# A convolution in the Winograd manner: the first block's outer taps and the parameters loaded through GpSimd's queue

## The chip, the cores and the metric

The kernel runs on one core of a Trainium2 chip. The metric is the device time of one execution in microseconds (us). The engines are TensorE (PE; its weight loads are PEld), VectorE (DVE), ScalarE (ACT), GpSimd (POOL) and SyncE (SP), which issues most of the transfers. A transfer ("DMA") is issued by an engine into that engine's queue and carried out by 16 DMA engines. Memory beside the engines holds 128 rows (partitions).

## The reference

A 1-D convolution over the sequence with three taps, 1024 channels in and out, batch 2 and sequence 2048, then batch normalisation with given statistics, then SiLU. Cut to what matters:

```python
def reference(x, w, mean, var, g, b):          # x (2, 2048, 1024), w (3, 1024, 1024), bf16
    xp = jnp.pad(x, ((0, 0), (1, 1), (0, 0)))
    y = sum(jnp.einsum('bsc,cd->bsd', xp[:, k:k + S, :], w[k]) for k in range(3))
    inv_std = 1.0 / jnp.sqrt(var + 1e-5)
    y = (y - mean) * (g * inv_std) + b
    return _silu(y)
```

## The kernel before

**The method.** The convolution is done in tiles of 6 outputs from 8 inputs. Three steps make it up. First the input is transformed: each window of 8 positions becomes 8 values (`NJ`), by products with a small constant matrix `rm`. Then the taps are transformed: for each block of 128 output channels (`dc`, 0 to 7) the three taps `w0`, `w1`, `w2` become eight sets of weights; two of the eight are `w0` and `w2` as they are, the other six (`u`) are sums and differences of `w0`, `w2`, their multiples by 4, and `w1` or its double. Last, for each block and batch (a `Unit`), eight products over the 8 tiles of 128 input channels (`ct`) are added up in PSUM, and VectorE and ScalarE combine them into 6 outputs and apply scale, offset and SiLU.

**The input transform.** `load_x` (L99) loads one tile of 128 input channels of one batch, 512 KB; tiles 0 and 1 of the first batch come as two halves, the first half on SP's queue and the second on ScalarE's. There are `XBUFS` = 6 buffers. `Jobs.do` (L226) multiplies six or four windows at a time (16 windows a tile) at L231, and ScalarE (L249) or VectorE (L251) copies the result out of PSUM into `T_sb`. Which engine copies and which PSUM banks are used is written out by hand in `ORDER` (L29), which also says where products of the first unit (`First`, L398) are mixed in, and where a few products on zeros fill in (`z5`). `load_small` (L94) loads the 48 rows of input that the tiles leave over; for the second batch it is cut into 15, 26 and 7 rows.

**The taps of the first block.** `load_w` (L107) loads taps of one block into `raw[dc]`, laid out as three taps beside each other in each row. For block 0 it loads tap 0 and tap 2 as two transfers of 256 KB right behind input tile 2, and tap 1 behind input tile 7; other blocks come as one transfer of 768 KB. All are on SP's queue. GpSimd makes the six sets `u` of block 0: `prepare_first` (L167) first forms three sums `e` from `w0` and `w2` (L137, L129), then with tap 1 the six results (L150). `prepare_second` (L183) does block 1, with some help by ScalarE, and `prepare_w` (L152) the later ones.

**The scales.** `scales` (L206) stands ahead of that on GpSimd. It waits for the parameters `prm` (var, g, mean, b: 128 rows of 64 bytes, L524) and computes scale and offset with six operations on 8 elements a row, one of them a power (L211).

**The order.** Nothing is reordered by a scheduler: each engine runs its instructions in the order of the program. A transfer on SP's or ScalarE's queue also waits for the landing of the transfer eight issues before it in the two queues taken together, because eight completion counters are used in turn. Transfers on GpSimd's queue have counters of their own. On SP the order is: first half of tile 0, first half of tile 1, parameters, 48 rows left over, tile 2, tap 0, tap 2, tiles 3 to 7, tap 1, then the second batch. ScalarE's queue has `rm` and the two second halves.

Of the kernel before, what the change touches and what calls it, by code (L numbers as in the profile page):

```python
# [17 lines left out]
XBUFS = 6  # L18
LROWS = 48
SROW = 66  # L20
NTILES = 342
NBP = 384

# [1 line left out]

BANKS = {"A": 4, "B": 6, "C": 2, "D": 0}
ORDER = (  # L29
    "Aa Ba Cd Da Ad Ba s2d z5 Da Bd Ca Da Bd Aa Cd Da Aa Bd Da Cd Aa Bd 3 Ca 2 Aa Bd 2 Ca 2 Aa 2 Bd "  # L30
# [6 lines left out]
def kernel(  # L37
# [53 lines left out]
    small = xlpool.tile([P, CT * P], BF16, name="xl")  # L91
    nc.vector.memset(small, 0.0)

    def load_small(bi, cuts=()):  # L94
        cuts = (0, *cuts, LROWS)
        for lo, hi in zip(cuts, cuts[1:]):
            nc.sync.dma_start(out=small[bi * SROW + lo:bi * SROW + hi], in_=xl[bi, lo:hi])

    def load_x(bi, ct, parts=1, second=nc.scalar):  # L99
        t = xpool.tile([P, NF, P], BF16, name="xw")  # L100
        xt[bi, ct] = t
        step = NF // parts
        for q in range(parts):
            s = slice(q * step, (q + 1) * step)
            (second if q else nc.sync).dma_start(out=t[:, s], in_=x[bi, ct, :, s])

    def load_w(dc, taps):  # L107
        if dc not in raw:
            raw[dc] = wpools[dc // 2 % 2].tile([P, 3, CT, P], BF16, name=f"wch{dc // 2 % 2}")
        if len(taps) == 3:  # L110
            nc.sync.dma_start(out=raw[dc], in_=w[dc])
        else:
            for k in taps:
                nc.sync.dma_start(out=raw[dc][:, k], in_=w[dc, :, k])

# [6 lines left out]
    def scaled(src, by, eng):  # L124
        t = spool.tile([P, CT, P], BF16, name="w1x2")
        if eng is nc.scalar:
            nc.scalar.mul(t, src, by)
        else:
            eng.tensor_scalar(t, src, by, 0.0, op0=ALU.mult, op1=ALU.add)  # L129
        return t  # L130

    def double_w(dc, eng):
        double[dc] = scaled(raw[dc][:, 1], 2.0, eng)

    def even(dc, q, a, b):
        sums[dc, q] = epool.tile([P, CT, P], FP32, name=f"e{q}")
        nc.gpsimd.tensor_tensor(sums[dc, q], a, b, op=ALU.add)  # L137

    def even_vector(dc, q):
        w0, w2 = raw[dc][:, 0], raw[dc][:, 2]  # L140
        sums[dc, q] = e = epool.tile([P, CT, P], FP32, name=f"e{q}")
        f, h = (w2, w0) if q == 1 else (w0, w2)
        nc.vector.scalar_tensor_tensor(out=e, in0=f, scalar=4.0, in1=h, op0=ALU.mult, op1=ALU.add)  # L143

    def transform_w(dc, q, signs=(0, 1)):
        o = double[dc] if q else raw[dc][:, 1]
        if (dc, q) not in wts:
            wts[dc, q] = upool.tile([P, 2, CT, P], BF16, name=f"u{q}")
        for i in signs:
            nc.gpsimd.tensor_tensor(wts[dc, q][:, i], sums[dc, q], o, op=(ALU.add, ALU.subtract)[i])  # L150

    def prepare_w(dc):  # L152
        even(dc, 0, raw[dc][:, 0], raw[dc][:, 2])
        transform_w(dc, 0)

        def second():
            even_vector(dc, 1)
            transform_w(dc, 1)

        def third():  # L160
            even_vector(dc, 2)
            transform_w(dc, 2)

        act_work.append(lambda: double_w(dc, nc.scalar))
        dve_work.extend((second, third))

    def prepare_first(dc):  # L167

        w0, w2 = raw[dc][:, 0], raw[dc][:, 2]

        def evens():
            even(dc, 0, w0, w2)
            even(dc, 1, scaled(w2, 4.0, nc.gpsimd), w0)
            even(dc, 2, scaled(w0, 4.0, nc.gpsimd), w2)

        def left():
            double_w(dc, nc.gpsimd)
            for q, i in ((0, 0), (1, 0), (0, 1), (1, 1), (2, 0), (2, 1)):
                transform_w(dc, q, (i,))

        return evens, left

    def prepare_second(dc):  # L183
        w0, w2 = raw[dc][:, 0], raw[dc][:, 2]

        def first():
            even(dc, 0, w0, w2)
            transform_w(dc, 0)

        def second():  # L190
            even(dc, 1, scaled(w2, 4.0, nc.scalar), w0)

        def third():
            double_w(dc, nc.scalar)
            transform_w(dc, 1)

        def fourth():
            even(dc, 2, scaled(w0, 4.0, nc.scalar), w2)
            transform_w(dc, 2)

        return first, second, third, fourth
# [4 lines left out]
    def scales():  # L206
        mhalf = consts.tile([P, DC], FP32, name="mhalf")
        nc.gpsimd.memset(mhalf, -0.5)
        sc = consts.tile([P, DC], FP32, name="sc")
        nc.gpsimd.tensor_scalar(sc, prm[:, 0, :], 1e-5, 1.0, op0=ALU.add, op1=ALU.mult)  # L210
        nc.gpsimd.tensor_tensor(sc, sc, mhalf, op=ALU.pow)  # L211
        nc.gpsimd.tensor_tensor(sc, prm[:, 1, :], sc, op=ALU.mult)
        nc.gpsimd.tensor_tensor(beta, prm[:, 2, :], sc, op=ALU.mult)
        nc.gpsimd.tensor_tensor(beta, prm[:, 3, :], beta, op=ALU.subtract)
        nc.gpsimd.tensor_scalar(scale, sc, 1.0 / 36.0, 0.0, op0=ALU.mult, op1=ALU.add)
# [47 lines left out]
    class Unit:  # L263
# [6 lines left out]
        def product(self, q, j, add, between):  # L270
            dc = self.dc
            nsl = slice(self.lo, self.hi)
            for ct in range(CT):
                between()
                if j == 0 or j == NJ - 1:
                    lhsT = raw[dc][:, 0 if j == 0 else 2, ct]
                else:
                    lhsT = wts[dc, (j - 1) // 2][:, (j - 1) % 2, ct]
                nc.tensor.matmul(  # L279
                    self.bank[q], lhsT=lhsT, rhs=T_sb[self.bi][:, ct, j, nsl],  # L280
                    start=not add and ct == 0, stop=ct == CT - 1, skip_group_check=add,
                )
# [90 lines left out]
    class First(Unit):  # L373
# [18 lines left out]
        def do(self):  # L392
            j, q, add, ct = self.todo.pop(0)
            if j == 0 or j == NJ - 1:
                lhsT = raw[self.dc][:, 0 if j == 0 else 2, ct]
            else:
                lhsT = wts[self.dc, (j - 1) // 2][:, (j - 1) % 2, ct]
            nc.tensor.matmul(  # L398
                self.bank[q], lhsT=lhsT, rhs=T_sb[self.bi][:, ct, j, :],
                start=not add and ct == 0, stop=ct == CT - 1, skip_group_check=True,  # L400
            )
            if ct == CT - 1:
                self.behind(j, q)
# [116 lines left out]


    load_x(0, 0, 2)
    load_x(0, 1, 2)
    nc.sync.dma_start(out=prm, in_=prm_in)  # L524
    load_small(0)
    scales()
    nc.scalar.activation(dummy[:, 1:2], dummy[:, 0:1], ACT.Silu)
    for ct in range(2, CT):
        load_x(0, ct)
        if ct == 2:  # L530
            load_w(0, (0, 2))
    load_w(0, (1,))
    load_x(1, 0, 2, nc.sync)
    load_small(1, (15, 41))
    for ct in range(1, CT):
        load_x(1, ct)
    load_w(1, (0, 1, 2))

# [26 lines left out]
    prev = unit  # L567
    xscope.close()
    wpools.append(ctx.enter_context(tc.tile_pool(name="wpool1", bufs=2)))
    load_w(2, (0, 1, 2))  # L570
    load_w(3, (0, 1, 2))
    for i, (dc, bi) in enumerate(seq[1:-1], 1):
        unit = Unit(dc, bi, i % 2 * 4)
        also = prev.rest(quiet)
        if i == 1:
            also = [(1, second[0]), (4, second[1])] + also
        if i == 2:
            also = prev.rest(quiet, 5, 4)
        if i == 3:
            also = also + [(1, lambda: idle(act_work)), (1, lambda: idle(dve_work))]  # L580
        if i == len(seq) - 2:
            also = prev.rest(quiet, 4, 5)
        unit.run(
            quiet, also,
            2 if i == 2 else dc + 2 if bi == 1 and 0 < dc < DC - 2 else None, i == 2, i == 1, i == 3,
        )
        if bi == 0 and dc + 3 < DC:
            load_w(dc + 3, (0, 1, 2))
        prev.store(nc.sync)
        prev = unit  # L590

# [29 lines left out]
def _laid_out(np, x, w, mean, var, g, b):  # L621


    B, S, C = x.shape
    K, _, D = w.shape
    CT, DC = C // P, D // P
    NF = S // (R * WT)
    step = R * WT
    xp = np.zeros((B, step * NF + P, C), x.dtype)
    xp[:, 1:S + 1] = x  # L630
    wins = np.stack([xp[:, f * step:f * step + P] for f in range(NF)], 2)
    wins = wins.reshape(B, P, NF, CT, P).transpose(0, 3, 1, 2, 4)
    rm = np.zeros((P, NJ, WT), np.float32)
    for n in range(WT):
        rm[R * n:R * n + NJ, :, n] = np.array(_POINTS, np.float32).T
    return (
        wins,
        xp[:, step * NF:step * NF + LROWS],
        w.reshape(K, CT, P, DC, P).transpose(3, 2, 0, 1, 4),
        np.stack([var, g, mean, b]).reshape(4, DC, P).transpose(2, 0, 1),  # L640
        rm.astype(x.dtype),
    )
# [30 lines left out]
```

## Time and profile before

| what | value |
|---|---|
| median of 3 runs | 181.75 us (181.59 to 182.36) |
| the profiled execution | 181.6 us, of which the span of the profile is 179.8 |
| busy: PE, DVE, POOL, ACT | 96%, 82%, 78%, 62% of the span |
| transfers | 24.58 MB, mean 137 GB/s; 373 to 417 GB/s in the slices from 4.5 to 27 us |
| granted clock of TensorE | 0.999 |

The page gives the busy share of each engine, a picture of the span in 40 slices of 4.5 us, the chain of work that ended last, and the costliest groups of instructions. Times in a timeline are in us from the start of the span: start, duration, engine, line, operation, result and operands, and in brackets the idle time of the engine before it and what ended it. Lines such as L231 are those of the code above. In the chain of waits the columns are start, duration and what held the chain in that time; "DMA xw" there is the landing of an input tile. The trace also records when each of the engines' shares of a transfer landed; the landing of a transfer is the last of these.

### The profile page before, as it was taken

How to read it: one execution, taken by the hardware profiler on the slowest of the kernel's cores; microseconds unless marked ns; L12 is line 12 of the kernel's file. 1: busy time of each engine (PE TensorE's matmuls, PEld its weight loads, DVE VectorE, ACT ScalarE, POOL GpSimd, SP SyncE). 2: the span in 40 equal slices, each digit the busy share in tenths (PEclk: the TensorE clock that was granted, in tenths of full speed). 3: DMA queues.
4: the chain of work that ended last, by engine and by line, in shares of the span. 5: the costliest groups of instructions: out<-in, count | busy, mean ns of one | idle time of the engine just before them, and what ended most of it. 6: DMA issues, size and time to landing. Idle time of an engine off the chain costs nothing.

```text
span 179.8 us, 3491 instructions
## 1 busy us (share of the span) xinstructions
PE 173.3 (96%) x1372; PEld 124.4 (69%) x1372; DVE 148.2 (82%) x193; ACT 110.8 (62%) x175; POOL 140.6 (78%) x77
## 2 busy tenths in 40 slices
PE   7889999999999999999999999999999999999991
PEld 5768888766666666666666666666666666668891
DVE  1568788987969999998898989898998997766792
ACT  3779989968364747365545654555456454573774
POOL 2499999999997979999999999999979978000000
PEclk9999999999999999999999999999999999999999
DMA  5999993170325030823073306430303020213033
GB/s 161 373 415 380 401 417 132 51 303 4 131 79 231 0 131 0 225 86 131 0 177 133 131 0 127 183 131 2 128 7 131 0 112 25 87 44 128 8 142 121
DMA packets 7507, 24.58 MB, mean 137 GB/s; under 512 B 1123, under 2 KB 1635, under 8 KB 7491
## 3 DMA queue, kind: packets, MB, share of 16 engines
q1 hardware_dynamic: 6915, 23.74, 36.1%
q10 hardware_dynamic: 576, 0.63, 1.0%
q8 instruction: 10, 0.16, 0.4%
q14 instruction: 6, 0.05, 0.1%
HBM read 14.93 MB, written 9.44 MB: 136 GB/s over the span
## 4 chain that ended last, share of the span: by engine, by line
PE 88%; DMA 5%; DVE 3%; ACT 1%; issue 0%; ACTq 0%; DVEq 0%
PE ps L279 75%; PE ps L231 8%; DMA xw<-in_x_dram 5%; PE ps L398 5%; DVE ps L294 2%; DVE t L294 1%; ACT yh L298 1%; ACT T_sb L249 1%; ACTq L78 0%; DVEq L662 0%; DVE sd L294 0%; PE ps L240 0%; PE ps L596 0%; DVEq L294 0%
## 5 line engine op out<-in xcount | busy, mean ns | idle before, releaser
L279 PE MATMUL ps<-T_sb,u 128*128 128x342 bf16 (+2 forms) x768 | 109.4, 298 | 0.0
L279 PEld LDWEIGHTS <-u 128*128 128x128 bf16 x768 | 72.2, 97 | 32.8 <-POOL u L150 0.3
L150 POOL TENSOR_TENSOR u<-e,w1x 128x1024 bf16<-128x1024 f32 x32 | 71.5, 2259 | 5.6 <-DVE e L143 5.5
L279 PE MATMUL ps<-T_sb,wch 128*128 128x342 bf16 (+2 forms) x256 | 39.5, 299 | 0.4 <-DVE ps L294 0.4
L294 DVE SCALAR_TENSOR_TENSOR t<-ps,sd 128x684 f32<-128x684 f32 (+2 forms) x49 | 37.6, 819 | 0.6
L298 ACT ACTIVATE yT<-ps,beta,scale 128x342 bf16<-128x342 f32 (+1 forms) x42 | 29.1, 727 | 12.6 <-PE ps L279 12.6
L150 POOL TENSOR_TENSOR u<-e,wch 128x1024 bf16<-128x1024 f32 x16 | 35.7, 2247 | 0.5
L279 PEld LDWEIGHTS <-wch 128*128 128x128 bf16 x256 | 24.2, 97 | 11.1 <-issue 0.5
L288 ACT COPY pc<-ps 128x342 f32<-128x342 f32 (+2 forms) x32 | 13.6, 424 | 28.4 <-PE ps L279 25.7
L249 ACT CAST T_sb<-ps 128x1008 bf16<-128x1008 f32 (+1 forms) x32 | 27.3, 879 | 3.9 <-PE ps L231 3.5
L251 DVE CAST T_sb<-ps 128x1008 bf16<-128x1008 f32 (+2 forms) x18 | 19.3, 1094 | 9.7 <-PE ps L231 9.2
L294 DVE SCALAR_TENSOR_TENSOR ps<-ps,t 128x684 f32<-128x684 f32 (+2 forms) x32 | 26.5, 829 | 0.7
L294 DVE SCALAR_TENSOR_TENSOR ps<-ps,pc 128x342 f32<-128x342 f32 (+2 forms) x34 | 16.9, 497 | 12.1 <-PE ps L279 8.8
L231 PE MATMUL ps<-rm,xw 128*128 128x168 bf16 x256 | 23.4, 239 | 1.6 <-DMA xw<-in_x_dram 1.4
L143 DVE SCALAR_TENSOR_TENSOR e<-wch 128x1024 f32<-128x1024 bf16 x12 | 24.6, 2052 | 0.0
L231 PEld LDWEIGHTS <-xw 128*128 128x128 bf16 x256 | 19.9, 99 | 4.8 <-DMA xw<-in_x_dram 2.4
L137 POOL TENSOR_TENSOR e<-wch 128x1024 f32<-128x1024 bf16 x8 | 19.0, 2372 | 0.1
L298 ACT ACTIVATE yT<-t,beta,scale 128x684 bf16<-128x684 f32 x15 | 14.4, 958 | 0.0
L294 DVE SCALAR_TENSOR_TENSOR t<-ps,t 128x684 f32<-128x684 f32 (+2 forms) x17 | 13.9, 817 | 0.0
L288 ACT COPY sd<-ps 128x342 f32<-128x342 f32 (+2 forms) x16 | 6.8, 426 | 10.3 <-PE ps L279 9.3
L290 ACT ACTIVATE pc<-ps 128x342 f32<-128x342 f32 (+2 forms) x16 | 7.0, 438 | 8.8 <-PE ps L279 6.1
L294 DVE SCALAR_TENSOR_TENSOR sd<-pc,ps 128x342 f32<-128x342 f32 (+2 forms) x17 | 8.2, 484 | 4.1 <-ACT sd L288 4.0
(45 smaller groups left out, 67.3 us busy)
## 6 DMA issues: line engine op xcount, KB each, us to landing
out_dram<-yT SPq DMA_DIRECT2D x15, 576.0 KB, 2.8
xw<-in_x_dram SPq DMA_DIRECT2D x13, 512.0 KB, 6.4
wch<-in_w_dram SPq DMA_DIRECT2D x7, 768.0 KB, 5.5
xw<-in_x_dram SPq DMA_DIRECT2D x4, 256.0 KB, 8.4
wch<-in_w_dram SPq DMA_DIRECT2D x3, 256.0 KB, 5.2
xw<-in_x_dram ACTq DMA_DIRECT2D x2, 256.0 KB, 4.6
out_dram<-yh SPq DMA_DIRECT2D x1, 256.0 KB, 2.0
out_dram<-yh SPq DMA_DIRECT2D x1, 128.0 KB
```

Source lines behind the costliest of these rows:

```text
L137: nc.gpsimd.tensor_tensor(sums[dc, q], a, b, op=ALU.add)
L143: nc.vector.scalar_tensor_tensor(out=e, in0=f, scalar=4.0, in1=h, op0=ALU.mult, op1=ALU.add)
L150: nc.gpsimd.tensor_tensor(wts[dc, q][:, i], sums[dc, q], o, op=(ALU.add, ALU.subtract)[i])
L231: nc.tensor.matmul(src[:, q // per, q % per], lhsT=xt[bi, ct][:, f + q], rhs=rm, start=True, stop=True)
L249: nc.scalar.copy(dst, src)
L251: nc.vector.tensor_copy(dst, src)
L279: nc.tensor.matmul(self.bank[q], lhsT=lhsT, rhs=T_sb[self.bi][:, ct, j, nsl], start=not add and ct == 0, stop=ct == CT - 1, skip_group_che ...
L288: nc.scalar.copy(dst, self.bank[q])
L290: nc.scalar.mul(dst, self.bank[q], by)
L294: nc.vector.scalar_tensor_tensor(out=out, in0=in0, scalar=scalar, in1=in1, op0=ALU.mult, op1=op1)
L298: nc.scalar.activation(self.yT[:, rows, self.y0:self.y0 + self.hi - self.lo], src, ACT.Silu, bias=beta[:, dc:dc + 1], scale=scale[:, dc:dc ...
L398: nc.tensor.matmul(self.bank[q], lhsT=lhsT, rhs=T_sb[self.bi][:, ct, j, :], start=not add and ct == 0, stop=ct == CT - 1, skip_group_check ...
```

## The change

- The parameters are loaded right behind the first tile, ahead of the second: rows 0 to 118 on GpSimd's queue, rows 119 to 127 on SP's. GpSimd issues its part ahead of `scales`.
- The taps are laid out in memory in the order 0, 2, 1, so that taps 0 and 2 are 4 KB side by side in a row. For block 0 their rows 0 to 119 are one transfer on GpSimd's queue, issued inside `scales` behind the first operation on the parameters and ahead of the power; rows 120 to 127 are one transfer on SP's queue behind tile 2.
- `load_small` no longer cuts the second batch's 48 rows into three.

On SP the order is now: first half of tile 0, 9 rows of parameters, first half of tile 1, 48 rows left over, tile 2, 8 rows of taps 0 and 2, tiles 3 to 7, tap 1, the second batch. On GpSimd: memsets, 119 rows of parameters, first operation of the scales, 120 rows of taps 0 and 2, the power and the other four operations, then the sums `e`.

```diff
+PROWS = 119
+WROWS = 120
+W0, W2, W1 = range(3)
...
-    def load_small(bi, cuts=()):
-        cuts = (0, *cuts, LROWS)
-        for lo, hi in zip(cuts, cuts[1:]):
-            nc.sync.dma_start(out=small[bi * SROW + lo:bi * SROW + hi], in_=xl[bi, lo:hi])
+    def load_small(bi):
+        nc.sync.dma_start(out=small[bi * SROW:bi * SROW + LROWS], in_=xl[bi])
...
-    def load_w(dc, taps):
+    def load_w(dc, taps=slice(0, 3), rows=slice(0, P), queue=nc.sync):
...
-        if len(taps) == 3:
-            nc.sync.dma_start(out=raw[dc], in_=w[dc])
-        else:
-            for k in taps:
-                nc.sync.dma_start(out=raw[dc][:, k], in_=w[dc, :, k])
+        queue.dma_start(out=raw[dc][rows, taps], in_=w[dc, rows, taps])
...
         nc.gpsimd.tensor_scalar(sc, prm[:, 0, :], 1e-5, 1.0, op0=ALU.add, op1=ALU.mult)
+        load_w(0, slice(W0, W1), slice(0, WROWS), nc.gpsimd)
         nc.gpsimd.tensor_tensor(sc, sc, mhalf, op=ALU.pow)
...
     load_x(0, 0, 2)
+    nc.sync.dma_start(out=prm[PROWS:], in_=prm_in[PROWS:])
+    nc.gpsimd.dma_start(out=prm[0:PROWS], in_=prm_in[0:PROWS])
     load_x(0, 1, 2)
-    nc.sync.dma_start(out=prm, in_=prm_in)
     load_small(0)
     scales()
...
         if ct == 2:
-            load_w(0, (0, 2))
-    load_w(0, (1,))
+            load_w(0, slice(W0, W1), slice(WROWS, P))
+    load_w(0, slice(W1, W1 + 1))
     load_x(1, 0, 2, nc.sync)
-    load_small(1, (15, 41))
+    load_small(1)
...
-        w.reshape(K, CT, P, DC, P).transpose(3, 2, 0, 1, 4),
+        w[[0, 2, 1]].reshape(K, CT, P, DC, P).transpose(3, 2, 0, 1, 4),
```

Everywhere else the indices 0, 1 and 2 of the taps become the names `W0`, `W1` and `W2`, and the loads of whole blocks are written `load_w(dc)`.

## The prediction

> **What bounds the kernel now.** I read the chain of waits first: it says which engine owns which stretch of time.
>
> ```profile
> 1.16 4.56 DMA xw<-in_x_dram
> 5.74 5.05 DMA xw<-in_x_dram
> 10.83 2.33 PE ps L231 x28
> 13.16 0.02 issue
> 13.19 1.01 ACT T_sb L249
> 14.19 0.04 issue
> 14.24 1.76 PE ps L231 x22
> ...
> 37.50 126.70 PE ps L279 x872
> ```
>
> Up to 10.83 us the kernel waits for input transfers, to 14.24 for ScalarE's evictions, and from there TensorE works without a break: 872 products in 126.70 us are 145 ns each. A change of the start-up is therefore worth what it moves 14.24, unless something later is bound by another engine. The timeline of GpSimd and TensorE shows one such place:
>
> ```profile
> 1.46 0.10 POOL L208 MEMSET mhalf<- 128x8 f32 x1
> 6.51 0.20 POOL L210 TENSOR_SCALAR sc<-prm 128x8 f32<-128x8 bf16 x1 [4.95 <-DMA prm<-in_prm_dram]
> 6.79 1.66 POOL L211 TENSOR_TENSOR sc<-sc,mhalf 128x8 f32<-128x8 f32 x1
> ...
> 9.36 0.20 POOL L215 TENSOR_SCALAR scale<-sc 128x8 f32<-128x8 f32 x1
> 9.66 2.12 POOL L137 TENSOR_TENSOR e<-wch 128x1024 f32<-128x1024 bf16 x1
> ...
> 46.91 4.23 POOL L150 TENSOR_TENSOR u<-e,w1x 128x1024 bf16<-128x1024 f32 x2
> ```
>
> ```profile
> 49.09 0.41 PEld L279 LDWEIGHTS <-u 128*128 128x128 bf16 x4 [0.33 <-POOL u L150]
> ```
>
> From 9.66 to 51.1 GpSimd never idles, and at 49.09 TensorE waits for it: two products start 0.29 us apart where 0.145 is usual. So a second chain, 0.15 us longer than the first, runs from GpSimd's start on the taps (9.66) to 49.09. Write dP for what the change moves 9.66, dT for what it moves 14.24. The end moves by the larger of dP and dT - 0.15. Both chains must move for a gain; a loss in either counts.
>
> Next, what decides 9.66 and 10.83. From the trace's landing records: x of tile 2 landed at 8.25, tap 0 at 8.88, tap 2 at 9.51, x of tile 3 at 10.78. The parameters landed at 6.43, and six small operations behind them ended at 9.56. So 9.66 has two causes within 0.05 us, the scale arithmetic and tap 2, and the change touches both.
>
> The rate of the transfers, in windows of 1 us (last three columns: granted clock, DMA share, GB/s):
>
> ```profile
> 5.00:6.00 1.00, 0.47 (x6) 0.24 (x5) 0.00 (x0) 0.99 (x1) 0.00 (x0) 1.00 1.07 378
> 6.00:7.00 1.00, 1.00 (x17) 1.00 (x15) 0.44 (x1) 0.73 (x1) 0.41 (x2) 1.00 0.96 303
> 7.00:8.00 1.00, 1.00 (x18) 0.77 (x15) 0.91 (x2) 1.00 (x2) 1.00 (x1) 1.00 1.01 393
> 8.00:9.00 1.00, 0.86 (x15) 0.87 (x12) 1.00 (x2) 0.79 (x2) 0.84 (x3) 1.00 1.08 424
> ```
>
> The engines stand at their share of about 1 from 4 us on, moving 378, 303, 393, then 424 GB/s. What stands in the queue, not when SP issues it, sets the landings.
>
> **The change, part by part.**
>
> *SP's queue.* The parameters' issue shrinks to 9 rows and moves from third to second place; one issue of 8 rows takes the place of two of 256 KB.
>
> ```profile
> 2.56 0.42 SPq L105 DMA_DIRECT2D xw<-in_x_dram  x1
> 3.93 0.80 SPq L114 DMA_DIRECT2D wch<-in_w_dram  x2
> 5.74 2.39 SPq L105 DMA_DIRECT2D xw<-in_x_dram  x5
> ```
>
> Each transfer of SP and ScalarE waits for the one eight before it: tap 0 for the matrix (3.91), tile 3 for the second half of tile 0 (5.72). In the changed order tile 3 waits for the first half of tile 0 (3.75) and for SP, which issues the 8 rows at 3.93; it goes out at about 4.3, not 5.74. This 1.4 us buys nothing by itself: the queue did not run dry at 5.74. What counts is that 512 KB of taps, 1.27 us at the 512 KB per 1.27 us of the landings from 9.51 on, no longer stand ahead of tile 3 in that queue. They go through the same 16 engines from another one, so the bytes ahead of tile 3 fall only if they come later. At 11 us the sum is unchanged. The 9 rows put 0.42 us ahead of tile 1's first half, whose issue moves from 1.15 to 1.6; its packets start at about 3.0, when tile 0's half is through (128 packets): hidden.
>
> *Issues on GpSimd.* No row shows GpSimd issuing a transfer. From below, its shortest row is 0.10 us; from above, its longest row of 8 elements is 1.66. SP's row of 128 descriptors is 0.42. GpSimd does it by program, as it does its arithmetic, so I take 1.0 an issue and keep both ends. The first stands at 1.5 us, in a wait of 4.95: free. The second stands between two scale operations and counts in full.
>
> *The parameters.* The nearest row for small packets beside large ones is the matrix on ScalarE's queue: 128 rows of 336 bytes, issued 0.72, landed 3.91, so 3.2 us; the fastest from above is the last stores' 1.5 us. From 1.5 with 1.0 of issue this gives 4.0 to 5.7 us; I take 4.6 against 6.43. The 9 rows lie behind tile 0's first half, which landed at 3.75. Then: first operation 4.7 to 4.9, issue of the taps to 5.9, power 1.66 to 7.6, four operations at 0.28 to 8.75 (they ended at 9.56).
>
> *The taps.* First packets came 1.0 us after the start of an issue at the first transfer (0.72 to 1.7), about 0.5 after its end, so 6.4 here. Each engine has 8 rows of 4 KB at 159 ns. When ScalarE's and SP's queues were both full (4.5 to 5.0 us) the packet records count 78 data packets of the one and 87 of the other: queues take turns packet by packet. 8 rows then take 8 x 2 x 0.159 = 2.5 us: 8.9, landed at 9.2. Tile 2 had about 5 rows left at 6.4; 5 turns go to the taps, 0.8 us, and it lands at 9.1, not 8.25. The 8 rows on SP stand right behind it, one row on each of eight engines: 9.3, landed about 9.5. Tile 3 has the same bytes ahead of it: 10.8.
>
> *Sum.* dP: the later of 8.75 and 9.5, plus 0.05, against 9.66: -0.1. dT: tile 2's products start at 9.15 instead of 8.63, and ScalarE has this cover:
>
> ```profile
> 9.26 1.62 ACT L249 CAST T_sb<-ps 128x1008 bf16<-128x1008 f32 x2 [0.47 <-PE ps L231]
> 11.47 5.29 ACT L249 CAST T_sb<-ps 128x1008 bf16<-128x1008 f32 x6 [0.59 <-PE ps L231]
> ```
>
> 9.8 + 1.62 = 11.45, just in time for 11.47. The cover of 0.59 is used up; if tile 2 came 0.3 us later still, 14.24 would move by 0.3. So dT is 0 (-0.1 to +0.3). The end moves by -0.1. Profiled execution: 181.6 (span 179.8 and 1.8 around it), so 181.5; the median shown, 181.75, is 0.15 above it: 181.6.
>
> *The rest.* Three small loads of the second batch's remainder (15, 26 and 7 rows) become one. They landed by 19.71 and are used at 23.0: nothing. The taps' new order changes addresses only. The second batch's tiles keep their bytes; tile 1 of it landed at 20.68 and is first used at 21.0. That 0.33 us limits any gain too.
>
> A rule speaks against the change: the Trainium skill, DMA: Bandwidth & Descriptors, section "Issuing engines are not separate DMA queues", says that transfers of all engines share the same 16 DMA engines and a second issuer saves issue time only. The windows (share about 1 from 4 us) agree; by the rule alone dT and dP would be 0.
>
> **The rivals.**
>
> 1. *The new queue fills the gaps* (18%). Against 424 GB/s, the stretch from 5 to 8 us lacks 198 KB, 0.47 us. If one queue alone could not keep the engines fed there and two can, tiles 2 and 3 land 0.45 earlier, dP is -0.5, dT -0.45: 181.0. For it: 303 GB/s at a share of 0.96. Against it: the share was not lower, so packets were slow rather than missing. Filling 3 to 5 us too would give another 0.5 and pass 0.5%; half of its chance goes there.
>
> 2. *The taps come late, and GpSimd's chain carries it to 49.09* (14%). If the parameters land no earlier than 6.43, the first operation ends at 6.7, the issue at 7.7, packets run from 8.2 at half rate to 10.75, landed 11.0. dP is +1.4, and the whole of it arrives, since the chain has no slack: 182.9 to 183.1. It decides once the taps land after 9.65, and passes 0.5% after 10.5.
>
> 3. *The power operation does not move* (10%). It took 1.66 us where its neighbours of the same size take 0.20; twice before it, at 1.5, GpSimd changes its configuration (MODIFY_POOL_CONFIG). If the 1.66 is the end of a load that began there, the power ends 6.95 us after that point whatever the parameters do, and the issue now ahead of it, 1.0 us, shifts it to 9.4: scales end at 10.5, dP +0.9: 182.4. The Trainium skill, GPSIMD Engine Reference, section "2.1 Instruction dispatch", gives such a first call about 6 us; no run here shows it by itself.
>
> 4. *VectorE holds up GpSimd's issue* (4%). Casts run from 6.56 to 9.18 without a break. If the issue falls there and waits for their end, packets run from 9.7 to 12.2: dP +2.8, 184.4. The Trainium skill, SBUF — State Buffer, section "SBUF: two separate sides", describes this trap: while VectorE runs an operation in a two-port mode, GpSimd cannot write its descriptors. Against it: a cast of 1008 elements takes 1.21 us, over 1 ns an element, no fast mode.
>
> 5. *Nothing reaches the end, or the change has no effect on landings*: that is the forecast itself (54%), 181.1 to 182.2.
>
> **Numbers.** 0.5% is 0.9 us, about what a measurement of this kernel tells from no change. Forecast 54%, rivals 18, 14, 10 and 4. Faster by over 0.5%: half of rival 1, 9%. Slower: rivals 2 and 4 and a third of 3, 21%. Within: 70%. The range for 8 in 10 goes just past rival 1's 181.0 and up to rival 2's 183.1.
>
> **What would show it.** Right: parameters used before 5 us; first `e` of GpSimd at 9.3 to 9.7; tile 2's products near 9.1; 14.24 and 49.09 unmoved within 0.3. Wrong: first `e` after 10.5 (rivals 2 to 4: late first operation, a power operation over 1.7 us, or an issue that ends after a cast), or tile 3's products before 10.4 (rival 1). A cost outside the span would be seen as a growth of the 1.8 us.

## The result and the profile after

The changed kernel takes **189.07 us** (median of 4 runs, 188.28 to 189.33) against 181.69 for the one before (4 runs on the same chip): a ratio of 1.039 [1.035, 1.043]. The profiled execution took 188.91, its span is 187.1 us: 7.3 more than before, and the 1.8 us around the span have not grown. So the loss stands inside the trace.

The chain of waits of the kernel after (start, duration, what held the chain):

```profile
1.47 5.10 DMA prm<-in_prm_dram
6.90 8.68 DMA wch<-in_w_dram
15.65 2.12 POOL e L135
...
25.42 2.10 POOL u L148
27.56 1.45 PE ps L397 x7
...
44.66 126.53 PE ps L278 x872
```

Before, this chain began with input tiles and TensorE. Now it is GpSimd's: parameters, taps, arithmetic, and only at 27.56 TensorE. The last line is the same 872 products in the same time (126.70 before). They start at 44.66 instead of 37.50: the whole loss, 7.16 us, lies ahead of them.

GpSimd's timeline of the kernel after:

```profile
1.47 0.78 POOL L523 DMA_DIRECT2D prm<-in_prm_dram  x1
...
6.65 0.19 POOL L208 TENSOR_SCALAR sc<-prm 128x8 f32<-128x8 bf16 x1 [4.28 <-DMA prm<-in_prm_dram]
6.90 0.55 POOL L112 DMA_DIRECT2D wch<-in_w_dram  x1
7.47 1.69 POOL L210 TENSOR_TENSOR sc<-sc,mhalf 128x8 f32<-128x8 f32 x1
...
10.07 0.20 POOL L214 TENSOR_SCALAR scale<-sc 128x8 f32<-128x8 f32 x1
15.65 2.12 POOL L135 TENSOR_TENSOR e<-wch 128x1024 f32<-128x1024 bf16 x1 [5.38 <-DMA wch<-in_w_dram]
```

The scales are done at 10.27, and then GpSimd stands idle for 5.38 us, for taps it had asked for at 6.90. Its first `e` starts at 15.65, not 9.66: dP is +5.99. The trace's packet records cut the 8.68 us of the taps in two: the first data packet at 10.9, 4.0 after the start of the issue, and then 4.7 to the landing at 15.58. The parameters went the same way: issue at 1.47, first packets 3.5 later, landed at 6.57.

The windows of the kernel after (last three columns: granted clock, DMA share, GB/s) show the taps' stretch:

```profile
10.00:11.00 1.00, 0.64 (x9) 0.50 (x7) 0.58 (x2) 1.00 (x2) 0.20 (x1) 1.00 1.02 406
11.00:12.00 1.00, 0.88 (x10) 0.74 (x10) 0.66 (x1) 0.94 (x2) 0.00 (x0) 1.00 1.07 328
12.00:13.00 1.00, 1.00 (x17) 1.00 (x15) 0.65 (x1) 0.99 (x2) 0.00 (x0) 1.00 1.02 279
13.00:14.00 1.00, 0.86 (x11) 0.57 (x8) 1.00 (x2) 0.85 (x2) 0.00 (x0) 1.00 1.04 270
14.00:15.00 1.00, 0.00 (x0) 0.00 (x0) 0.67 (x1) 1.00 (x2) 0.00 (x0) 1.00 1.02 287
```

The share of busy time stays about 1 while the rate falls from 406 to 270 GB/s as soon as the taps run: packets of 4 KB take 235 ns at the median, on GpSimd's queue and on SP's alike, where they took 159 before. The 8 rows on SP's queue are not behind it: they had landed at 9.32, and from 9.3 to 10.8 us the rate was 407 GB/s. A share of 1 tells that engines are occupied, not that they move much.

TensorE's timeline of the kernel after, where the late taps reach it, and the windows around it:

```profile
23.31 1.32 PE L230 MATMUL ps<-rm,xw 128*128 128x168 bf16 x16
27.56 1.45 PE L397 MATMUL ps<-T_sb,u 128*128 128x342 bf16 x7 [2.93 <-POOL u L148]
28.81 0.52 PE L239 MATMUL ps<-rm,xl 128*128 128x48 bf16 x8
29.16 1.85 PE L230 MATMUL ps<-rm,xw 128*128 128x168 bf16 x12
```

```profile
24.40:27.50 3.10, 0.23 (x4) 0.02 (x1) 1.21 (x1) 1.16 (x2) 3.10 (x4) 1.00 1.03 407
...
28.40:31.80 3.40, 3.40 (x29) 2.87 (x27) 1.24 (x2) 1.00 (x1) 3.40 (x3) 0.50 0.58 237
```

The same place in TensorE's timeline of the kernel before:

```profile
20.84 1.32 PE L231 MATMUL ps<-rm,xw 128*128 128x168 bf16 x16
22.00 1.18 PE L398 MATMUL ps<-T_sb,u 128*128 128x342 bf16 x7
```

The first `u` is used at 27.56, before at 22.00: 5.56 later (5.99 less the slack that `u` had). TensorE's last product ahead of it started at 24.39, 3.2 us earlier; the profile, which models where products end, counts 2.93 us of idle time. That last product started at 21.93 before, so TensorE's own chain was 2.46 us late as well, hidden behind the later `u`. Behind the wait the granted clock reads 0.50 for 3.4 us. Work at half speed for 3.4 us loses 1.7; 5.56 and 1.6 make the 7.16.

### The profile page after: what moved, and what is told of

It reads as the page before. It is cut to its first block, busy times and chain, and to the rows that moved or that the text cites. A ratio compares the mean times of both kernels' runs of the same rounds, so it can differ in the third digit from the quotient of the medians.

```text
span 187.1 us, 3492 instructions
## 1 busy us (share of the span) xinstructions
PE 174.8 (93%) x1372; PEld 125.4 (67%) x1372; DVE 148.6 (79%) x193; ACT 111.0 (59%) x175; POOL 140.8 (75%) x79
## 4 chain that ended last, share of the span: by engine, by line
PE 80%; DMA 7%; POOL 7%; DVE 3%; ACT 1%; issue 1%; DVEq 0%; POOLq 0%
PE ps L278 72%; DMA wch<-in_w_dram 5%; PE ps L230 4%; PE ps L397 4%; POOL e L135 3%; DMA prm<-in_prm_dram 3%; POOL w1x L127 2%; DVE ps L293 2%; POOL u L148 1%; DVE t L293 1%; ACT yh L297 1%; POOL yT L260 0%; DVEq L662 0%; PE ps L239 0%; DVE sd L293 0%
## 5 line engine op out<-in xcount | busy, mean ns | idle before, releaser
L148 POOL TENSOR_TENSOR u<-e,w1x 128x1024 bf16<-128x1024 f32 x32 | 69.4, 2192 | 7.8 <-DVE e L141 6.4
L148 POOL TENSOR_TENSOR u<-e,wch 128x1024 bf16<-128x1024 f32 x16 | 36.5, 2300 | 0.6
L248 ACT CAST T_sb<-ps 128x1008 bf16<-128x1008 f32 (+1 forms) x32 | 27.4, 878 | 10.9 <-PE ps L230 10.6
L230 PE MATMUL ps<-rm,xw 128*128 128x168 bf16 x256 | 24.2, 243 | 4.2 <-DMA xw<-in_x_dram 3.7
L230 PEld LDWEIGHTS <-xw 128*128 128x128 bf16 x256 | 20.6, 101 | 7.9 <-DMA xw<-in_x_dram 4.9
L141 DVE SCALAR_TENSOR_TENSOR e<-wch 128x1024 f32<-128x1024 bf16 x12 | 25.3, 2110 | 0.0
L397 PE MATMUL ps<-T_sb,u 128*128 128x342 bf16 x48 | 10.0, 322 | 2.9 <-POOL u L148 2.9
```

The costliest lines, as they stand in the source:

```text
L230: nc.tensor.matmul(src[:, q // per, q % per], lhsT=xt[bi, ct][:, f + q], rhs=rm, start=True, stop=True)
L248: nc.scalar.copy(dst, src)
L397: nc.tensor.matmul(self.bank[q], lhsT=lhsT, rhs=T_sb[self.bi][:, ct, j, :], start=not add and ct == 0, stop=ct == CT - 1, skip_group_check ...
```

## The experiments

The theory after the result: GpSimd's chain carries the loss, as rival 2 had it, in three parts: (i) the first packet of a GpSimd transfer comes 3 to 4 us after the start of its issue, (ii) a transfer of 120 rows makes packets slow, its own and those beside it, (iii) a long wait of TensorE halves its clock. Rivals: the parameters' path is to blame rather than the taps'; VectorE holds GpSimd's issue up; the new place in SP's order is to blame; the delay (i) is fixed, or belongs to the start-up, or to the load on the DMA engines.

**1. The parameters' part alone** (the taps whole on SP):

```diff
-        load_w(0, slice(W0, W1), slice(0, WROWS), nc.gpsimd)
...
-            load_w(0, slice(W0, W1), slice(WROWS, P))
+            load_w(0, slice(W0, W1))
```

> The changed kernel, but taps 0 and 2 of block 0 go whole (128 rows, 512 KB) by SP's queue behind tile 2; only the 119 rows of parameters stay on GpSimd's queue. Theory A (delay): a transfer on GpSimd's queue sends its first packet about 3.5 us after its issue begins, so the parameters land at 6.4 to 6.7 as before, the taps at about 9.4, the first sum e starts at 9.5 to 9.8: 181.3 to 182.2 us. Theory B (sharing): only bulk data on GpSimd's queue costs anything: the same time, parameters not fixed. If the parameters on GpSimd's queue are what costs, over 184.

Measured: 1.0026 [1.0002, 1.005], span 180.9. The lines of its GpSimd timeline and, last, of TensorE's:

```profile
7.28 0.19 POOL L208 TENSOR_SCALAR sc<-prm 128x8 f32<-128x8 bf16 x1 [4.91 <-DMA prm<-in_prm_dram]
...
10.40 2.12 POOL L135 TENSOR_TENSOR e<-wch 128x1024 f32<-128x1024 bf16 x1
```

```profile
49.88 1.34 PE L277 MATMUL ps<-T_sb,u 128*128 128x342 bf16 x8 [0.44 <-POOL u L148]
```

Put first in program order but on GpSimd's queue, the parameters landed at 7.19, later than from third place on SP (6.43). dP is +0.74, and TensorE waits at 49.88 instead of 49.09: +0.79 (the span grew by 1.1, the time by some 0.5 by the ratio). The second chain that the prediction found is real and has no slack. This run also has SP's new order and the new order of the taps in memory, so neither is to blame for the 7 us.

**2. The taps' part alone** (the parameters whole on SP, third as before):

```diff
-    nc.sync.dma_start(out=prm[PROWS:], in_=prm_in[PROWS:])
-    nc.gpsimd.dma_start(out=prm[0:PROWS], in_=prm_in[0:PROWS])
     load_x(0, 1, 2)
+    nc.sync.dma_start(out=prm, in_=prm_in)
```

> The changed kernel with the parameters back on SP's queue as one transfer in third place; the taps stay on GpSimd's queue behind the first scale operation. Theory A: the parameters land at about 6.4, the issue begins at about 6.8, first packets at 10.4, the taps land at 15 to 15.6: 188 to 189.3 us, no better than the changed kernel. Theory B: the same. If the two transfers of GpSimd hold each other up, first packets before 9 and under 187 us.

Measured: 1.035 [1.031, 1.040]. The taps were issued at 6.51, first packet 4.3 us later, landed 15.14, `e` at 15.21. Almost the whole loss is the taps'; the parameters add little.

**3. The taps' issue moved up**, right behind that of the parameters, with no wait ahead of it:

```diff
+        load_w(0, slice(W0, W1), slice(0, WROWS), nc.gpsimd)
         nc.gpsimd.tensor_scalar(sc, prm[:, 0, :], 1e-5, 1.0, op0=ALU.add, op1=ALU.mult)
-        load_w(0, slice(W0, W1), slice(0, WROWS), nc.gpsimd)
```

> The changed kernel with the issue of the taps moved up to stand right behind that of the parameters, so that it waits for nothing and begins at about 2.4 us. Theory A (a fixed delay of 3.5 us, met twice in series): first packets at 5.9, with about 4.4 us of sharing they land at 10 to 11, e starts at 10 to 11, the first u at 22 to 23: 181.9 to 183.2 us. Theory B (sharing the 16 engines with SP's loads is the cost, not the delay): the stretch from first packet to landing stays over 4.5 us and the loads of SP slip with it, over 184. Theory C (VectorE's casts keep GpSimd from writing descriptors): no casts run from 2.4 to 5, so first packets before 4.5 and landing by 9.

Measured: 1.018 [1.013, 1.023]: about half of the loss is gone, less than theory A expected; the time and the slow, long transfer are those of theory B. Issue at 2.29, first packet 3.1 later, but 241 ns a packet, so landed only at 11.55 and `e` at 11.65. Tile 2 shares the engines with it and landed at 11.74 (8.25 before): TensorE stood from 9.52 to 11.78 and ran at half clock for 3.4 us from 13.2 on. Here TensorE's chain decides: dP is +2.0, but the first `u` is used at 26.02, right behind the product before it, 4.0 later than before, and the span grew by 4.1.

**4. The long wait filled** with 30 products on zeros:

```diff
-Ba 7
+Ba z30 7
```

> The changed kernel with 30 small products on zeros put where TensorE waits 3.17 us for the first transformed taps. They add work and no result. Theory A's last term: of the 7.3 us about 5.6 are the late taps and 1.6 to 1.7 a lowered granted clock behind that wait; with the wait filled the clock stays at 1.0 and the time falls to 187.1 to 187.7 us. Rival: the 1.6 us come from elsewhere (VectorE, ScalarE or GpSimd behind their buffers): 188.6 or more, with the clock at 1.0.

Measured: 1.034 [1.032, 1.037], span 186.4. In its windows the clock behind the filled wait stays at 1.00, and half a clock appears elsewhere, behind the wait for tile 5:

```profile
13.70:15.80 2.10, 0.22 (x4) 0.01 (x1) 1.04 (x1) 1.49 (x2) 0.00 (x0) 1.00 1.01 295
16.10:19.50 3.40, 3.40 (x27) 3.40 (x25) 2.06 (x2) 1.59 (x2) 3.25 (x3) 0.50 1.05 378
...
28.10:31.50 3.40, 3.40 (x43) 2.87 (x42) 1.57 (x2) 1.50 (x2) 3.40 (x2) 1.00 0.81 330
```

Here `e` came 0.37 and the first `u` 0.53 later than in the kernel after (16.02, 28.09), yet the span is 0.6 shorter: the filled wait saved about 1.1. The time, 188.34, lies above the 187.1 to 187.7 that was expected, and its interval touches that of the kernel after. That the clock takes a part of the loss is shown by the rows: 43 products in the 3.4 us behind the filled wait, 29 in the kernel after. How large the part is, 1.1 or 1.7, rests on one trace each.

**5. All 128 rows** in GpSimd's transfer, none on SP:

```diff
-WROWS = 120
+WROWS = P
...
-            load_w(0, slice(W0, W1), slice(WROWS, P))
```

> The changed kernel with all 128 rows of taps 0 and 2 in the one transfer on GpSimd's queue and none on SP's. Theory A1 (it is the 120 rows: consecutive rows put on 15 engines write where other engines write): with 128 rows the packets of the two queues take about 160 ns each instead of 230, the taps land 2.2 to 2.6 us after their first packet instead of 4.5 to 5, at about 13.3, and the time falls to 186 to 187.3 us. Theory A2 (two queues of 4 KB packets from GpSimd and SP slow each other whatever the rows): packets stay at 220 to 260 ns, 188.3 to 189.3 us.

Measured: 1.034 [1.026, 1.041]. The same windows as above, of this kernel:

```profile
11.00:12.00 1.00, 1.00 (x15) 0.91 (x13) 0.14 (x1) 0.65 (x1) 0.00 (x0) 1.00 1.05 430
12.00:13.00 1.00, 0.64 (x7) 0.46 (x6) 1.00 (x1) 0.98 (x2) 0.00 (x0) 1.00 1.01 414
13.00:14.00 1.00, 0.88 (x14) 0.88 (x13) 0.31 (x2) 0.96 (x1) 0.00 (x0) 1.00 1.03 418
```

Eight rows more, and the packets take 159 ns on both queues, at 414 to 430 GB/s instead of 270 to 328. So (ii) holds for the packets. The 8 rows that this run also leaves out seem to cost a little too: from 8 to 9 us, while they were under way, the kernel after moved 328 GB/s, this one 422. `e` starts at 14.55, 1.1 earlier, though the issue was 0.2 later. The median, 188.50, is only some 0.6 below that of the kernel after, inside the noise and above the 186 to 187.3 that was expected: the wait and the half clock behind it (27.8 to 31.2) remain. The packets decide here, not the time.

**6. The taps on ScalarE's queue**, 128 rows behind its half of tile 1, the parameters whole on SP in second place, nothing on GpSimd's (only the added lines):

```diff
+    nc.sync.dma_start(out=prm, in_=prm_in)
     load_x(0, 1, 2)
     load_small(0)
+    load_w(0, slice(W0, W1), queue=nc.scalar)
```

> The same plan without GpSimd's queue: the parameters whole on SP in second place, taps 0 and 2 as one 512 KB transfer of 128 rows on ScalarE's queue behind the second half of tile 1. Theory A (GpSimd's queue costs the delay of 3 to 4 us; sharing between two hardware queues costs nothing): first packets of the taps by 5.5, packets near 160 ns, landing at 7.5 to 9, e at 7.6 to 9.1, tile 2 at 9 to 9.5, and 181.3 to 182.3 us. Theory B (two queues at once run below one alone, whichever): packets of 220 ns or more, tile 2 after 10, over 183.5 us.

Measured: 1.0058 [1.0021, 1.0094], span 180.7. Parameters landed at 4.26, taps at 8.40, `e` at 8.47: dP is -1.2. But tile 2 landed at 9.67 (8.25), and TensorE passed ScalarE's wait at 14.97 instead of 14.24. dT is +0.73, and the span grew by 0.9: the taps' gain is the tiles' loss, and the larger of the two shifts decides. The median, 182.74, is a little above the 181.3 to 182.3 of theory A; the landings are as it had them.

**7. 120 and 8 rows on SP's queue**, otherwise as the first experiment:

```diff
-            load_w(0, slice(W0, W1))
+            load_w(0, slice(W0, W1), slice(0, WROWS))
+            load_w(0, slice(W0, W1), slice(WROWS, P))
```

> As the first experiment (parameters split, taps on SP behind tile 2), but the taps as 120 rows and 8 rows, both on SP's queue. Theory A1 (120 rows are slow by themselves): packets over 200 ns in that transfer, landing 1 us or more later than the 9.8 of the first experiment, 182.8 us or more. Theory A2: landing at 9.7 to 10.3, packets near 160 ns, 181.8 to 182.6 us.

Measured: 1.0099 [1.0064, 1.0134]. Between 8 and 11.5 us half of its packets take 263 to 319 ns, its windows read 236 and 218 GB/s at a share of 1.03 and 1.02, and `e` starts at 12.12 where the first experiment had 10.40. The cost of 120 and 8 rows is not GpSimd's: it follows the shape of the transfer.

**8. VectorE left idle** through the first three tiles, its casts given to ScalarE:

```diff
-    "Aa Ba Cd Da Ad Ba s2d z5 Da Bd Ca
+    "Aa Ba Ca Da Aa Ba s2a z5 Da Ba Ca
```

> The changed kernel with VectorE's casts of the first three tiles given to ScalarE, so that VectorE does nothing from 1.7 to about 12 us; ScalarE has more to do, and that may cost time of its own. Theory A (fixed delay): the issue of the taps at about 7 still has its first packet 3.5 to 4 us later, near 10.7, and they land at 15 to 16. Theory C (VectorE's casts hold up the descriptors): first packets 1.5 us after the issue, near 8.5, and landing before 13.5.

Measured: 1.042 [1.039, 1.046]. VectorE had no cast until 13.23; the taps were issued at 7.77, and their first packet still came 3.84 us after that. The prediction's rival 4 falls.

**9. Loads in the quiet part.** The kernel before, with five loads into a tile that nothing reads, put where hardly anything else is transferred (cut to the core):

```diff
+    probes = {5: (nc.gpsimd, P, 0), 7: (nc.gpsimd, 120, 2), 9: (nc.gpsimd, P, 2), 11: (nc.sync, 120, 2), 13: (nc.sync, P, 2)}
...
+                queue.dma_start(out=probe[0:rows], in_=w[0, 0:rows, 0:2])
```

> The kernel before, with five extra loads into an unused tile in the steady part, where the transfers stand still most of the time: on GpSimd's queue 119 rows of 64 bytes, 120 rows of 4 KB and 128 rows of 4 KB, on SP's queue 120 and 128 rows of 4 KB. Nothing waits for them. It measures the two disputed costs by themselves. Theory A: from the start of the issue to the first packet 3 to 4 us on GpSimd's queue and about 1 on SP's, with idle DMA engines as well; 120 rows take 200 ns or more a packet on either queue, 128 rows 160. Rival (the delay is the queue of SP's packets already waiting in the DMA engines at the start): about 1 to 1.5 us on GpSimd's queue here.

Measured: 1.0025 [1.0003, 1.0046]. On GpSimd's queue, from start of issue to first packet: 1.47 us for 119 rows of 64 bytes, 1.25 for 120 rows of 4 KB, 1.31 for 128; to the landing 2.12, 4.43 and 3.69. The fixed delay of 3 to 4 us that I had taken over from the result **fell**. With nothing else moving, the 120 rows had a median of 159 ns a packet, but a mean of 217, against 159 and 177 for 128 rows, and took 3.18 us from the first packet to the landing against 2.39. So most of the cost of 120 rows shows beside another transfer, and a part of it remains alone. The two probes on SP's queue ran beside stores of results: a median of 168 and a mean of 228 ns for 120 rows, 159 and 189 for 128. SP's first packet came 0.97 us after the issue where its queue was empty.

**10. The repair of the issue's place**: 128 rows of taps as GpSimd's first instruction, parameters whole on SP in second place (only the added lines):

```diff
+    load_w(0, slice(W0, W1), queue=nc.gpsimd)
...
+    nc.sync.dma_start(out=prm, in_=prm_in)
     load_x(0, 1, 2)
```

> The plan with both costs taken out: taps 0 and 2 as 128 rows on GpSimd's queue, issued as GpSimd's first instruction (about 0.7 us) so that the delay lies under the loads of tiles 0 and 1; the parameters whole on SP in second place. Theory A: first packets at 4 to 4.8, landing at 7.2 to 8.5, parameters at 3.9 to 4.5, e at 7.5 to 8.6 (dP -1 to -2), tile 2 at 9 to 9.6 (dT 0 to +0.8): 181.4 to 182.6 us. If the delay of GpSimd's queue grows with what SP and ScalarE have queued, landing after 9.5 and 182.5 or more.

Measured: 1.0188 [1.0158, 1.0218], missed by far. GpSimd's side went about as expected:

```profile
1.22 0.77 POOL L112 DMA_DIRECT2D wch<-in_w_dram  x1 [0.79 <-POOLq L650]
...
8.17 2.12 POOL L137 TENSOR_TENSOR e<-wch 128x1024 f32<-128x1024 bf16 x1 [0.79 <-DMA wch<-in_w_dram]
```

dP is -1.5. TensorE's side did not, as the timeline and the windows show:

```profile
8.34 2.00 PE L231 MATMUL ps<-rm,xw 128*128 128x168 bf16 x13 [2.61 <-DMA xw<-in_x_dram]
```

```profile
8.30:11.60 3.30, 3.26 (x28) 2.92 (x29) 1.29 (x2) 1.72 (x2) 3.15 (x3) 0.50 1.02 406
```

The two halves of tile 1 landed at 8.29 and 8.46 (5.53 and 6.77 before), TensorE waited 2.6 us for the first of them, and half a clock followed. Early taps take their share from the tiles that TensorE needs first.

**11. The parameters second on SP**, and nothing else changed from the kernel before:

```diff
+    nc.sync.dma_start(out=prm, in_=prm_in)
     load_x(0, 1, 2)
-    nc.sync.dma_start(out=prm, in_=prm_in)
```

> The kernel before with one change: the parameters' transfer, whole on SP's queue, moves from third to second place. The taps stay as they were. By the two chains: scales end 1.5 us or more earlier, e then starts when tap 2 has landed, at 9.5 to 9.7 (dP -0.1), dT 0: 181.4 to 182.0 us, not to be told from before. Rival: the packets of 64 bytes hold up tile 1 and with it TensorE: 182.2 or more.

Measured: 1.0013 [0.9995, 1.0031]. The parameters are used at 4.24 instead of 6.51, and `e` waits for tap 2:

```profile
9.72 2.12 POOL L137 TENSOR_TENSOR e<-wch 128x1024 f32<-128x1024 bf16 x1 [2.44 <-DMA wch<-in_w_dram]
```

The parameters alone are worth nothing, as the prediction's two causes for 9.66 said.

**12. Both repairs together**: the taps' issue as in 3, 128 rows as in 5.

```diff
-WROWS = 120
+WROWS = P
...
+        load_w(0, slice(W0, W1), slice(0, WROWS), nc.gpsimd)
         nc.gpsimd.tensor_scalar(sc, prm[:, 0, :], 1e-5, 1.0, op0=ALU.add, op1=ALU.mult)
-        load_w(0, slice(W0, W1), slice(0, WROWS), nc.gpsimd)
...
-            load_w(0, slice(W0, W1), slice(WROWS, P))
```

> The changed kernel with two repairs together: 128 rows of taps instead of 120 and 8, and their issue right behind that of the parameters. Theory A, both costs taken from the changed kernel: first packets at 5.2 to 5.6, landing at 8 to 8.8, so e waits for the scales, whose parameters land on GpSimd's queue at 6.6 to 7.7: e at 9.8 to 11 (dP +0.2 to +1.3), tile 2 at 9.3 to 9.9: 182 to 183.3 us. If either repair undoes the other, over 184.5.

Measured: 1.0048 [1.0027, 1.0068], span 180.8. Issue at 2.28, first packet 3.3 later, 159 ns a packet, landed 9.70; `e` at 10.26 now waits for the scales. Issue place and row count together bring back 6.3 of the 7.3 us of span.

**13. The small load under load.** The kernel before, with six loads of 119 rows of 64 bytes on GpSimd's queue (the load alone, without its six places):

```diff
+    def probe():
...
+        nc.gpsimd.dma_start(out=t[0:119], in_=prm_in[0:119].rearrange("p a b -> p (a b)"))
```

> The kernel before with six added loads of 119 rows of 64 bytes on GpSimd's queue, each into a tile of its own that nothing reads: one ahead of the scales (about 1.5 us), one behind the first and one behind the second sum e of block 0 (about 12 and 16), and three among the six u of block 0 (about 24 to 35, the last when SP's loads of the second batch are through, at about 28). What is read is the time from the start of each issue to its first packet. Theory C (the delay follows the load on the 16 DMA engines, which SP's queue keeps busy until about 28 us): 2.5 to 4.3 us in the probes up to 25 us, 1.2 to 1.6 us in those after 28. Rival D (the delay belongs to the first seconds of the queue or of the start-up): 2.5 to 4.3 us in the first probe alone, 1.2 to 1.6 us in all later ones, though SP's queue is still full. The six issues of about 0.8 us each delay GpSimd's chain by up to 3.9 us ahead of 49.1, so the time is expected at 184.5 to 186.5 us and tells nothing by itself.

Its GpSimd timeline:

```profile
1.47 0.67 POOL L215 DMA_DIRECT2D probe<-in_prm_dram  x1
...
11.60 0.65 POOL L215 DMA_DIRECT2D probe<-in_prm_dram  x1
...
15.52 0.58 POOL L215 DMA_DIRECT2D probe<-in_prm_dram  x1
...
24.55 0.58 POOL L215 DMA_DIRECT2D probe<-in_prm_dram  x1
...
29.30 0.53 POOL L215 DMA_DIRECT2D probe<-in_prm_dram  x1
...
34.01 0.53 POOL L215 DMA_DIRECT2D probe<-in_prm_dram  x1
```

From these starts to the first packet: 3.14, 3.84, 2.95 and 3.50 us while SP's transfers run, 1.22 and 1.22 behind them (the rate is 376 GB/s from 24.5 to 28.5 us, 12 from 29.3 to 31). So the delay goes with the load, not with the first use or the start-up: theory C holds, D falls. 184.29 against 182.32 in one run each, a little under what was expected.

## Why the prediction was wrong

**What held.** The two chains and their rule. GpSimd's chain has no slack at 49.1 (experiment 1: dP +0.74, wait +0.79), TensorE's decides when its shift is the larger (experiment 6: dT +0.73, span +0.9), and with neither moved nothing happens (experiment 11). The issue costs GpSimd 0.55 to 0.78 us, within the ends (0.10 to 1.66). The power operation moved with its input and took 1.69: rival 3 falls. No gap was filled by the second queue (rival 1). The 8 rows on SP landed at 9.32, forecast 9.5, tile 2 at 8.91, forecast 9.1, and tile 3 at 10.34, forecast 10.8, but that is luck: the forecast delayed them by packets of the taps from 6.4 on, and those came only from 10.9. What did delay tile 2 is not settled; with the 8 rows behind it and no taps moving yet it landed at 8.84 to 9.36 (after, experiments 2, 4 and 8), without them at 8.56 and 8.60 (experiments 1 and 5).

**What failed: dP, forecast -0.1, was +5.99.** The terms, in their order:

| step of the prediction | taken | measured | lost |
|---|---|---|---|
| the parameters' landing | 4.6 | 6.57 | 2.0 |
| taps: first packet after the start of the issue | 1.5 | 4.0 | 2.5 |
| taps: first packet to landing | 2.8 | 4.7 | 1.9 |

The first row carries over whole, since the issue of the taps stands behind the first operation (6.90 instead of 4.9). The three sum to 6.4, and 9.2 + 6.4 is the measured 15.6. The first two rows are one mistake, made in "The parameters" and "The taps". For the taps I took the time from issue to first packet from SP's first transfer, which had found the engines empty (1.0 us), and added only GpSimd's own longer issue. For the parameters I took the matrix (3.2 us from issue to landing), which was issued together with that first transfer, and the last stores (1.5): again rows of engines with little to do. Experiment 13 gives 1.2 us for such engines and 3 to 4 for loaded ones. That was a cost of a state (engines busy with another queue) for which the trace before had no row. The bounds from both sides for what follows the issue (1.5 to 3.2 us for the parameters, none for the taps) came from the empty state.

The third row is the step "queues take turns packet by packet: 8 x 2 x 0.159". The turns held in experiments 5 and 12, both with 128 rows at 159 ns. What failed is 159 ns: beside another transfer 120 rows cost 235 (experiment 5 against after; in experiment 7 on SP's queue 276 at the median). This part of the loss is the diff's choice of 120 and 8. The Trainium skill, DMA: Bandwidth & Descriptors, section "The descriptor swizzle", says that in a transfer of 128 rows each of the 16 DMA engines writes the rows behind one port of the memory. With 128 rows the runs agree that two transfers hardly disturb each other (159 ns at the median). That 120 rows break this order, so that two engines meet at one port, would fit the 235 ns beside another transfer, but no run here shows ports: this stays an argument.

**dT, forecast 0, was about +2.5** (24.39 against 21.93 for the last product ahead of the first `u`) and was only hidden by the larger dP. TensorE waited 1.65 us for tile 1, whose first half landed at 7.16 (5.53 before), and 1.62 for tile 5, which landed at 15.44 among the slow packets of the taps; of the first batch the forecast had looked no further than tile 3. In experiment 3 this chain decides. (The 11.45 in the sum for dT should read 11.42; nothing hangs on it.)

**The term that was missing: the clock.** A dP of +5.99 alone would give 5.6 at the first `u`; the other 1.6 is TensorE at half clock for 3.4 us behind its wait for `u`. Before, the profile's clock row reads 9 throughout, so nothing showed it. The Trainium skill, TensorE: Matmul & The Clock Gate, section "HAM oscillation — how this bites in real kernels", warns of idle gaps over about 3.4 us. Here idle times of 2.9 (after), 2.6 (experiment 10) and 1.9 us (experiment 4) were followed by half a clock, so the measurement decides. But the length alone does not tell: experiment 7 waited 2.3 us and kept the full clock.

```profile
13.15 1.04 PE L229 MATMUL ps<-rm,xw 128*128 128x168 bf16 x12 [2.30 <-DMA xw<-in_x_dram]
```

```profile
13.20:16.60 3.40, 3.19 (x39) 2.77 (x40) 2.37 (x3) 2.71 (x4) 3.25 (x3) 1.00 1.03 409
```

The clock records of the traces tell the two apart. In all fifteen traces the clock changes only at whole multiples of 3.41 us from the first record. Where TensorE idled for 1.9 us or more within one such step, the next step was at half clock; behind a step at full clock with 1.65 us or less of idle time it never was. Experiment 7's wait lies across the border of two steps (0.8 and 1.5 us), as does the wait for tile 5 in the kernel after (0.8 and 0.8), while the same wait in experiment 4 lies within one step. Where the half clock falls is thus partly chance.

**Rival 2** named the mechanism ("the taps come late, and GpSimd's chain carries it"), its first condition (parameters not before 6.43) and its decision point, and priced it at 182.9 to 183.1 by the same 1.5 us and 159 ns. Its price carried the forecast's two wrong terms, so the range shared them. With the 5.56 that the first `u` really lost, the same chain gives 181.6 + 5.6 = 187.2, and 188.8 with the clock's 1.6.

**Open.** Why GpSimd's first packet waits 2 to 3 us longer on loaded engines is not settled. SP's issues are no measure of it, since their packets queue behind SP's own. Whether the delay follows the depth of the queue or the mere presence of other traffic was not tried. Nor is it settled what makes 120 rows slow.

## What to carry to other kernels

Moving a transfer to another engine's queue moves its bytes among the same busy engines: what the one lands earlier, the other lands later (experiments 6 and 10), so ask which of the two sits on the chain that ends last. A duration from an empty machine is not a bound for a loaded one; price each stretch of a transfer (issue, issue to first packet, packets) in the state in which it will run. When a wait of TensorE grows by two microseconds or more, expect that 3.4 us at half clock may follow: in these runs it did whenever 1.9 us of the wait fell into one 3.41 us step of the clock.

## What the runs showed of the hardware

- GpSimd's transfers: issue 0.53 to 0.78 us whatever the size; issue to first packet 1.2 to 1.5 us with quiet DMA engines, 2.6 to 4.3 beside SP's transfers.
- 120 rows of 4 KB beside another transfer slowed the packets of both from 159 to 235 ns and more at the start-up, on GpSimd's and on SP's queue, at an unchanged share of busy time; alone their median was 159 and their mean 217 (177 for 128 rows).
- TensorE's clock changed only in steps of 3.41 us. A step with 1.9 us or more of idle time was followed by one at half clock, a step at full clock with 1.65 or less was not; in experiment 8, with a wait of 4.0 us, two steps (6.8 us) ran at half clock.
